# Gating the first weight slot once, norm means in single-pass matmuls, and a new order: a fused attention, GLU and SoLU kernel

## The chip, the cores and the metric

One core of one Trainium2 chip runs the whole program. The metric is the device time of one execution in microseconds; lower is better. TensorE (PE, with its weight loads PEld), VectorE (DVE), ScalarE (ACT), GpSimd (POOL) and the DMA engines work side by side and wait for each other by semaphores. SyncE (SP) only issues transfers.

## The reference, cut to what matters

```python
scores = q @ k^T / sqrt(64), masked to a window of 32 (half of the heads: dilated by 4)
attn = exp(scores - max) / (sum + 1e-9)
x = (attn @ v)                       # 4 x 8 heads x 576 x 64  ->  2304 tokens x 512
xn = x / sqrt(mean(x * x) + 1e-6) * rms_g
g = xn @ w_gate; val = xn @ w_val    # 512 x 1536
x = (g * sigmoid(g) * val) @ w_out   # 1536 x 512
h = x @ w_in                         # 512 x 1024
sm = exp(h - max) / (sum + 1e-9); solu = h * sm
ln = (solu - mean) / sqrt(var + 1e-6) * g_ln
out = ln @ w_out                     # 1024 x 512
```

The attention arrays are float32; the weight matrices and gains are float64, and the matrices reach the kernel as 64-bit words that it turns into fp32 itself.

## The kernel before, in words

The 2304 tokens are cut into nine tiles of 256 (`PIECES`, t = 0 to 8) and these into five parts (`PARTS`): tiles 0 and 1, tile 2, tiles 3 and 4, tiles 5 and 6, tiles 7 and 8. The hidden width 1536 is cut into twelve weight slots f of 128. Slot f brings three weight pieces of 128x512: gate (0), value (1), output (2).

**Weights** (`prepare`). A piece arrives as 64-bit words by one transfer of 512 KB (`fetch`, line 371). ScalarE shifts the exponent (`shifted`, line 386), VectorE takes low bits (`parts`, line 391) and joins both to fp32 (`joined`, line 395). ScalarE makes the fp32r high half (`halves`, a cast by the helper `put`, line 333) and VectorE or GpSimd subtracts it from the whole to get the low half (`lows`, helper `less`, line 342). The list `cuts` says which pieces are converted together: before, slots below `SINGLE` = 7 one by one, later slots all three as one 1536-wide step.

**Products.** A product of two fp32 arrays is three fp32r matmuls (`mm3`, lines 952 to 954): high x high, high x low, low x high. `mlp` makes g and vp (gate and value), then tanh, silu, product and the high and low halves of u, then y (the output product, accumulated over all slots). `VIRTUAL` lists its runs: entries 0 and 1 are slot 0 alone for tile 0 and tile 1 (256 columns each, so that tile 0 can start before tile 1 is ready), entry 2 is slots 1 to 11 for both (512 columns), entry 3 is tile 2, entry 4 tiles 3 and 4. Tiles 5 to 8 go through `joint`, a Strassen scheme of 512-column products whose operands are combined beforehand (`ewhole`, `ecomb`, `estore`: line 1240 is the combination, line 1244 its store). `second_stage` does the SoLU layer.

**Attention.** `pair` handles tiles 0 and 1 (scores lines 509 and 511, transposes 544, values 566), `attention` the later tiles (scores 639, transposes 675, values 695).

**Norms** (`rms`). Tiles 0 and 1 use small matmuls (line 820), a power on GpSimd, a diagonal and a spreading matmul (863). Tiles 2 to 8 square and add on GpSimd, then one fp32 matmul of a matrix of ones with the 128x256 sum gives each column's sum on all partitions (`mean`, line 827), then a Newton root on VectorE. `scale` (874, 879), `high` and `low` make the operands.

**What sets the order.** Each step is added to a `Plan` with a cost per engine, what it needs, the buffers that it takes and a due time. `Plan.order` plays the plan: it takes the engine that can start earliest, and on it, among the steps that can start within a small slack, the one that is due first. Each engine then runs its steps in that order, in its own in-order queue; SP issues transfers in the same way. `NUDGE` shifts the due times of single steps, `ENGINE` fixes the engine of some, `PACE` says behind which gate product a tile's attention may start. While GpSimd works, the plan charges VectorE for it: 0.45 of the GpSimd cost. From the joint products on TensorE's order is a written list (`line` in `second_stage`).

Up to planned time 75 us (`FILL`), the builder puts dummy matmuls (line 351, 256 columns of bf16 from a constant) into planned gaps of TensorE:

```python
filling[0] = int((at_ - free) / (0.13 if free else 0.25)) if at_ < FILL else 0
```

Of the kernel before, what the change touches and what calls it, by code (L numbers as in the profile page):

```python
# [7 lines left out]
F32 = mybir.dt.float32  # L8
F32R = mybir.dt.float32r
# [35 lines left out]
def groups_of(piece):  # L45
# [30 lines left out]
    else:  # L76
# [7 lines left out]
        for at, bt in ((128, b), (192, b2)):  # L84
# [12 lines left out]
HALVES = 1  # L97

# [4 lines left out]
SINGLE = 7  # L103
# [6 lines left out]
NUDGE = {('centred', (1, 1)): -15.5, ('copy', (1, 0)): 10, ('copy', (3, 1)): 11, ('copy', (4, 1)): 57,  # L110
         ('copy', (5, 0)): 32, ('copy', (7, 1)): 50, ('ecomb', 5): -17, ('eload', 9): 14, ('eps', 1): -41.9,
         ('eps', 3): 13, ('ewhole', 1, 0): -45, ('ewhole', 2, 1): 35, ('ewhole', 3, 0): 48, ('ewhole', 4, 0): 15,
         ('exps', (2, 1)): 57, ('g', 2, 8, 1): 24, ('gln',): 60, ('high', 0, 0): -27, ('high', 1, 0): 35,
         ('landed', 6): -22, ('load_qk', (1, 1)): -1.6, ('load_v', (0, 0)): 3.07, ('low', 0, 1): -43.6,
         ('low', 1, 0): 93, ('low', 1, 1): -32.8, ('masking', (2, 0)): -65, ('masking', (3, 1)): -22,
         ('masking', (4, 1)): 40, ('masking', (5, 0)): 13, ('masking', (6, 0)): -65, ('maximum', (1, 0)): -3,
         ('maximum', (1, 1)): -8.1, ('maximum', (2, 0)): -98, ('maximum', (3, 1)): -45, ('maximum', (5, 1)): 78,
         ('newton', 0, 2): 58, ('norm', (0, 1)): -0.8, ('norm', (2, 1)): 31, ('out', 2, 1, 0): -124,
         ('out', 2, 1, 1): 45.1, ('out', 2, 2, 0): 7.5, ('prod', 1, 0): 28, ('prod', 3, 0): 43, ('prod', 4, 3): 23,
         ('prod', 4, 7): 71, ('rmsg',): 14, ('scale', 0, 1): -35.9, ('scale', 1, 0): -11.5, ('scale', 1, 1): -38.4,  # L120
         ('scale', 1, 2): 0.08, ('scale', 1, 4): 1, ('scale', 2, 0): -5.5, ('scale', 2, 1): -25, ('scale', 2, 3): 49,
         ('scale', 3, 0): -11.4, ('scale', 3, 1): -38.8, ('scale', 3, 4): 43, ('silu', 3, 3): 17, ('silu', 3, 4): 46,
         ('square', 0, 0): 77, ('square', 0, 1): -34.9, ('square', 1, 1): -32.9, ('square', 1, 4): -10,
         ('square', 2, 1): -42.3, ('square', 3, 1): -29.9, ('sums', (1, 0)): -45, ('sums', (1, 1)): 44,
         ('tanh', 'c11', 0): 138, ('total', 2, 0): -12, ('total', 3, 0): -9.1, ('turned0', (0, 1)): -34,
         ('turned1', (0, 1)): -38, ('uhigh', 3, 4): -68, ('ulow', 4, 2): 88, ('ulow', 4, 4): 1, ('xcomb', 't3'): 35,
         ('xcomb', 't4'): 44, ('xlow', 't1', 1): 8, ((1, 0), 'lows', 0): 19, ((1, 0), 'lows', 1): 11,
         ((1, 0), 'shifted', 2): 33, ((1, 1), 'fetch', 0): 41, ((1, 1), 'fetch', 1): 12, ((1, 1), 'fetch', 2): 6,
         ((1, 1), 'joined', 0): 5.2, ((1, 1), 'joined', 2): -10, ((1, 1), 'lows', 2): -16.5,
         ((1, 1), 'parts', 1): 10, ((1, 1), 'parts', 2): 47.5, ((1, 1), 'shifted', 1): 91,  # L130
         ((1, 1), 'shifted', 2): 41, ((1, 10), 'fetch', 2): -33, ((1, 10), 'parts', 0): 23,
         ((1, 11), 'fetch', 0): -52, ((1, 11), 'fetch', 1): 31.9, ((1, 11), 'fetch', 2): -32,
         ((1, 11), 'lows', 0): 19.5, ((1, 11), 'parts', 0): 22.9, ((1, 2), 'fetch', 1): -5,
# [12 lines left out]

ENGINE = {('copy', (3, 0)): 'd', ('copy', (5, 0)): 'd', ('copy', (7, 0)): 'd', ('copy', (7, 1)): 'd',
          ('copy', (8, 1)): 'a', ('ecomb', 0): 'p', ('ecomb', 1): 'p', ('ecomb', 11): 'd', ('ecomb', 8): 'p',
          ((1, 4), 'lows', 0): 'p', ((1, 6), 'lows', 1): 'p'}

FILL = 75.0

# [1804 lines left out]
```

## Time and profile before

| | us |
|---|---|
| median of 3 runs (711.76 to 712.01) | 711.76 |
| the profiled execution | 712.27 |
| its span, first to last instruction | 710.2 |
| TensorE matmuls busy | 702.3 |
| VectorE, ScalarE, GpSimd busy | 509.4, 358.9, 135.5 |

The granted TensorE clock is 1.00 over the whole span. A matmul's recorded time includes its way through the pipeline, so two matmuls overlap in the records: what a matmul costs is read from the distance between two starts. An fp32 matmul shows as two records. Rows of the timeline merge instructions that follow each other with one line and shape.

### The profile page before, as it was taken

The page shows a single profiled execution, that of the slowest core. Times are in us where ns is not written, and L with a number is a line of the kernel's source. Part 1 is how long each engine was busy: PE and PEld are TensorE (multiplying, and loading weights), DVE is VectorE, ACT ScalarE, POOL GpSimd, SP SyncE. Part 2 cuts the span into 40 slices and gives each one's busy share as a digit, 9 for nine tenths or more (in the row PEclk, how much of TensorE's full clock was granted, in tenths as well). Part 3 has the DMA queues.
Part 4 walks back from the last instruction along what each step waited for, and adds up shares of the span by engine and source line. Part 5 has one row for each costly group of instructions (what it writes and reads, how often), then busy time and mean ns, then how long its engine had stood idle before and what let it go on. Part 6 is the DMA issues. An engine that isn't in the chain of part 4 may idle for free.

```text
span 710.2 us, 11738 instructions
## 1 busy us (share of the span) xinstructions
PE 702.3 (99%) x4533; PEld 593.3 (84%) x4533; DVE 509.4 (72%) x932; ACT 358.9 (51%) x769; POOL 135.5 (19%) x166
## 2 busy tenths in 40 slices
PE   8999999999999999999999999999999999999998
PEld 6788888899998888888888888888888888888887
DVE  5899899679585986668966766689677677665552
ACT  2976854344535554516655554355375555543440
POOL 0322432250506121110000000014044311010110
PEclk9999999999999999999999999999999999999999
DMA  9999433154368764403321112947032111000001
GB/s 336 401 407 354 133 101 118 64 185 141 134 225 293 276 206 141 141 7 125 123 72 37 52 60 97 344 139 220 1 119 75 60 60 45 30 16 30 30 30 45
DMA packets 42424, 97.21 MB, mean 137 GB/s; under 512 B 3841, under 2 KB 14081, under 8 KB 42369
## 3 DMA queue, kind: packets, MB, share of 16 engines
q1 hardware_dynamic: 40640, 93.33, 37.9%
q10 hardware_dynamic: 1728, 3.15, 1.2%
q8 instruction: 35, 0.57, 0.3%
q14 instruction: 21, 0.16, 0.1%
HBM read 72.87 MB, written 23.59 MB: 136 GB/s over the span
## 4 chain that ended last, share of the span: by engine, by line
PE 93%; DMA 5%; ACT 1%; DVE 1%; SPq 0%; issue 0%; ACTq 0%
PE y L952 7%; PE ca L1292 7%; PE y L954 7%; PE y L953 7%; PE o L1689 5%; PE o L1688 5%; PE o L1687 5%; PE g L952 4%; PE vp L952 4%; PE g L953 4%; PE g L954 4%; PE vp L954 4%; PE vp L953 4%; DMA raw<-w 3%; PE cd L1292 2%; PE cb L1292 2%
## 5 line engine op out<-in xcount | busy, mean ns | idle before, releaser
L342 POOL TENSOR_TENSOR w<-wf,w 128x512 fp32r<-128x512 f32 (+1 forms) x15 | 25.1, 1673 | 203.9 <-ACT w L333 203.9
L1687 PE MATMUL o<-w,lt 128*128 128x512 f32 (+1 forms) x152 | 58.9, 388 | 0.0
L1689 PE MATMUL o<-w,lt 128*128 128x512 f32 (+1 forms) x152 | 57.6, 379 | 0.0
L1688 PE MATMUL o<-w,lt 128*128 128x512 f32 (+1 forms) x152 | 57.5, 379 | 0.0
L952 PE MATMUL y<-uh,w 128*128 128x512 f32 (+1 forms) x148 | 53.2, 359 | 0.0
L954 PE MATMUL y<-uh,w 128*128 128x512 f32 (+1 forms) x148 | 51.7, 349 | 0.0
L953 PE MATMUL y<-uh,w 128*128 128x512 f32 (+1 forms) x148 | 51.7, 349 | 0.0
L660 ACT ACTIVATE s<-s,nm 128x64 f32<-128x64 f32 x120 | 40.1, 337 | 18.6 <-DVE nm L655 18.6
L333 ACT CAST w<-wf 128x512 fp32r<-128x512 f32 (+1 forms) x40 | 28.3, 728 | 25.5 <-DVE wf L395 11.5
L952 PE MATMUL g<-xh,w 128*128 128x512 f32 (+1 forms) x104 | 40.4, 389 | 0.0
L333 ACT CAST uh<-u 128x512 fp32r<-128x512 f32 (+1 forms) x37 | 19.9, 537 | 38.3 <-DVE u L996 37.7
L953 PE MATMUL g<-xl,w 128*128 128x512 f32 (+1 forms) x104 | 39.0, 375 | 0.2 <-DVE xl L342 0.2
L952 PE MATMUL vp<-xh,w 128*128 128x512 f32 (+1 forms) x100 | 39.0, 390 | 0.0
L954 PE MATMUL g<-xh,w 128*128 128x512 f32 (+1 forms) x104 | 38.9, 374 | 0.0
L954 PE MATMUL vp<-xh,w 128*128 128x512 f32 (+1 forms) x100 | 38.2, 382 | 0.0
L953 PE MATMUL vp<-xl,w 128*128 128x512 f32 (+1 forms) x100 | 38.1, 381 | 0.0
L805 POOL TENSOR_TENSOR sq<-x 128x256 f32<-128x256 f32 x28 | 17.8, 647 | 105.7 <-DVE x L337 61.6
L1655 POOL TENSOR_SCALAR st<-st 128x1 f32<-128x1 f32 x18 | 8.7, 484 | 140.5 <-ACT sq L1646 140.3
L992 DVE SCALAR_TENSOR_TENSOR u<-u,g 128x512 f32<-128x512 f32 (+1 forms) x37 | 21.5, 582 | 18.3 <-ACT u L986 18.3
L986 ACT ACTIVATE u<-g 128x512 f32<-128x512 f32 (+1 forms) x37 | 19.0, 514 | 27.9 <-PE g L954 27.2
L1689 PEld LDWEIGHTS o<-w,lt 128*128 128x128 f32 x152 | 28.6, 188 | 5.3
L342 DVE TENSOR_TENSOR lt<-tp,lt 128x512 fp32r<-128x512 f32 x36 | 23.2, 684 | 13.6 <-ACT lt L333 13.6
(290 smaller groups left out, 2056.5 us busy)
## 6 DMA issues: line engine op xcount, KB each, us to landing
raw<-w SPq DMA_DIRECT2D x36, 512.0 KB, 9.1
es<-ec SPq DMA_DIRECT2D x12, 512.0 KB, 3.1
sc<-es SPq DMA_DIRECT2D x12, 512.0 KB, 3.4
qk<-qk SPq DMA_DIRECT2D x7, 800.0 KB, 5.5
vt<-v SPq DMA_DIRECT2D x10, 512.0 KB, 5.6
wo<-w SPq DMA_DIRECT2D x9, 512.0 KB, 7.6
wst<-wo SPq DMA_DIRECT2D x9, 512.0 KB, 3.7
yT<-yo SPq DMA_DIRECT2D x16, 256.0 KB, 3.1
```

The source lines that it names most:

```text
L333: nc.scalar.copy(dst, src) if scale is None else nc.scalar.mul(dst, src, scale)
L342: ENG[e].tensor_tensor(dst, a, b, ALU.subtract)
L660: nc.scalar.activation(T[s_][:, i], T[s_][:, i], AF.Exp, bias=st["nm"][:, i:i + 1], accum_out=sm[:, i:i + 1])
L952: nc.tensor.matmul(acc, wh, xh, start=first, stop=False)
L953: nc.tensor.matmul(acc, wh, xl, start=False, stop=False)
L954: nc.tensor.matmul(acc, wl, xh, start=False, stop=last)
L986: return lambda e: nc.scalar.activation(new(up, ("u", v, f), [P, 512])[:, 0:n], T["g", v, f], AF.Tanh, scale=0.5)
L992: return lambda e: nc.vector.scalar_tensor_tensor(out=u_of(f), in0=u_of(f), scalar=1.0, in1=T["g", v, f], op0=ALU.add, op1=ALU.mult)
L1292: nc.tensor.matmul(acc(x), w, y, start=not more and j == 0 and n == 0, stop=j == 1 and n == 2, skip_group_check=True)
L1687: nc.tensor.matmul(o, lt[:, 0, k], w[:, 0], start=(k == 0), stop=False)
L1688: nc.tensor.matmul(o, lt[:, 0, k], w[:, 1], start=False, stop=False)
L1689: nc.tensor.matmul(o, lt[:, 1, k], w[:, 0], start=False, stop=(k == NF2 - 1))
```

## The change

Slot 0 gets no runs of its own any more. It joins the run of slots 1 to 11; its g and vp are done tile by tile (`by_piece`), its tanh, silu, product, halves and y once for 512 columns. The seven means of tiles 2 to 8 split the sum of squares into fp32r high (ScalarE) and low (GpSimd or VectorE) halves and use two fp32r matmuls. Slots 2 to 6 convert gate and value pieces as one 1024-wide step and the output piece apart; slots 0 and 1 stay in three, slots 7 to 11 in one. The mask matmul of `pair` becomes a step of its own. The plan's costs are adjusted, GpSimd's charge on VectorE is 0.45 only for steps that end in "low" or "lows" and 0.12 for others, and `NUDGE`, `ENGINE` and `PACE` are new lists.

```diff
-HALVES = 1
-SINGLE = 7
+APART, WIDE = 2, 7
+def cuts(f):
+    return [(0,), (1,), (2,)] if f < APART else [(0, 1), (2,)] if f < WIDE else [(0, 1, 2)]
...
-NUDGE = {('centred', (1, 1)): -15.5, ('copy', (1, 0)): 10, ('copy', (3, 1)): 11, ('copy', (4, 1)): 57,
+NUDGE = {('centred', (1, 1)): 39.5, ('copy', (1, 0)): 10, ('copy', (3, 1)): 11, ('copy', (4, 1)): 57,
...
+         ('ewhole', 4, 0): 15, ('ewhole', 5, 0): -132, ('ewhole', 5, 1): 103, ('exps', (2, 1)): 57,
+         ('g', 2, 8, 1): 24, ('gln',): 60, ('high', 0, 0): -6, ('high', 1, 0): 35, ('ident',): -462,
+         ('landed', 6): -116, ('load', 3): -176, ('load_qk', (1, 1)): -1.6, ('load_v', (0, 1)): 3,
+         ('load_v', (1, 0)): 6, ('low', 0, 1): -43.6, ('low', 1, 0): 93, ('low', 1, 1): -32.8, ('mask',): -119,
...
-          ('copy', (8, 1)): 'a', ('ecomb', 0): 'p', ('ecomb', 1): 'p', ('ecomb', 11): 'd', ('ecomb', 8): 'p',
-          ((1, 4), 'lows', 0): 'p', ((1, 6), 'lows', 1): 'p'}
+          ('ecomb', 2): 'p', ('ecomb', 5): 'p', ('ecomb', 7): 'd', ('ecomb', 8): 'p', ('high', 0, 0): 'a',
...
+          ((1, 2), 'lows', 1): 'p', ((1, 3), 'lows', 0): 'p', ((1, 4), 'lows', 0): 'p', ((1, 5), 'lows', 0): 'p',
+          ((1, 5), 'lows', 1): 'd', ((1, 7), 'lows', 0): 'p', ((1, 8), 'lows', 0): 'p'}
...
-PACE = {2: [(2, 3), (2, 2)],
-        3: [(2, 6), (2, 6)],
-        4: [(2, 8), (2, 10), (3, 1)],
-        5: [(3, 6), (3, 6)],
-        6: [(3, 9), (4, 0)],
-        7: [(4, 1), (4, 2)],
-        8: [(4, 3), (4, 4), (4, 6)]}
+PACE = {2: [(2, 0), (2, 7)],
+        3: [(2, 5), (2, 8)],
+        4: [(2, 2), (3, 1), (2, 7)],
+        5: [(3, 4), (3, 3)],
+        6: [(2, 3), (4, 2)],
+        7: [(3, 8), (3, 0)],
+        8: [(3, 6), (2, 0), (3, 10)]}
...
-VIRTUAL = [(0, 0, 256, range(HALVES)), (0, 256, 256, range(HALVES)), (0, 0, 512, range(HALVES, NF1)),
-           (1, 0, 256, range(NF1)), (2, 0, 512, range(NF1))]
+VIRTUAL = {2: (0, 0, 512, range(NF1)), 3: (1, 0, 256, range(NF1)), 4: (2, 0, 512, range(NF1))}
...
             if e == "p" and free["d"] > start:
-                free["d"] += 0.45 * cost
+                free["d"] += (0.45 if any(str(x).endswith(("low", "lows")) for x in name) else 0.12) * cost
...
         def mean(e):
             x = bank(a_mean, [P, TP], "ms")
-            nc.tensor.matmul(x, ones, T["sq", t, ks[0]], start=True, stop=True)
+            for h in range(2):
+                nc.tensor.matmul(x, ones_r, T["sqh" if h == 0 else "sql", t], start=h == 0, stop=h == 1)
+        def sum_high(e):
+            put(e, new(at, ("sqh", t), [P, TP], F32R, name="sqh"), T["sq", t, ks[0]])
+        def sum_low(e):
+            less(e, new(at, ("sql", t), [P, TP], F32R, name="sql"), T["sq", t, ks[0]], T["sqh", t])
...
+                    fill(T[key][:, 0:TP])
+                else:
+                    filling[0] = 3 * filling[0] // 4
+                    if v == 2 and filling[0] > 0:
+                        fill(psy.tile([P, 512], F32, tag="y00", name="warm")[:, 0:TP])
...
-                    alone = v == 4 and f == 0 and part == 0
+                    alone = f == 0 and (v == 2 or v == 4 and part == 0)
+                    if alone and part == 1:
+                        before = [("g", v, f, i)] + ([(key, v, f, 0)] if i else [])
```

## Rows read from the trace of the kernel before

**Rows 1.** The page, part 1: busy time (share of the span) and instructions
```profile
PE 702.3 (99%) x4533; PEld 593.3 (84%) x4533; DVE 509.4 (72%) x932; ACT 358.9 (51%) x769; POOL 135.5 (19%) x166
```

**Rows 2.** Stages: length; PE, PEld, DVE, ACT, POOL busy (instructions); PEclk, DMA share, GB/s
```profile
0.00:36.66 36.66, 32.41 (x410) 25.56 (x410) 24.67 (x55) 22.48 (x41) 6.26 (x15) 1.00 0.98 370
36.66:80.00 43.34, 43.34 (x295) 36.72 (x296) 41.28 (x64) 30.99 (x61) 12.33 (x9) 1.00 0.84 321
80.00:196.00 116.00, 116.00 (x992) 104.27 (x991) 91.63 (x157) 56.24 (x170) 39.32 (x41) 1.00 0.37 127
196.00:198.00 2.00, 1.47 (x13) 1.30 (x13) 1.90 (x6) 0.60 (x3) 0.00 (x0) 1.00 0.77 213
198.00:706.00 508.00, 508.00 (x2821) 424.64 (x2821) 349.45 (x652) 248.55 (x499) 77.60 (x102) 1.00 0.32 107
```

**Rows 3.** Stages, line 351 alone: length; PE, PEld busy (instructions); PEclk, DMA share, GB/s
```profile
29.18:36.66 7.48, 3.14 (x25) 2.32 (x25) 1.00 1.03 397
36.66:710.20 673.54, 0.00 (x0) 0.00 (x0) 1.00 0.36 124
```

**Rows 4.** Timeline of PE around one mean: start us, us, engine line op out<-in xcount
```profile
107.19 0.39 PE L953 MATMUL y<-uh,w 128*128 128x512 f32 x1
107.42 0.39 PE L954 MATMUL y<-uh,w 128*128 128x512 f32 x1
107.65 0.59 PE L827 MATMUL ms<-sq,ones 128*128 128x256 f32 x2
...
108.31 0.39 PE L953 MATMUL g<-xl,w 128*128 128x512 f32 x1
```

**Rows 5.** Timeline of PE, the last slot-0 products and the first of slot 1
```profile
39.52 0.28 PE L952 MATMUL y<-uh,w 128*128 128x256 f32 x1
...
40.96 0.40 PE L952 MATMUL g<-xh,w 128*128 128x512 f32 x1
```

**Rows 6.** Timeline of all engines, how tile 1 (the second token piece) becomes ready
```profile
33.22 1.66 DVE L879 SCALAR_TENSOR_TENSOR x<-x,rmsg,rs 128x256 f32<-128x256 f32 x4 [0.19 <-PE rs L863]
...
34.69 0.68 ACT L386 ACTIVATE raw<-raw 128x512 f32<-128x512 f32 x1 [0.38 <-DMA raw<-w]
...
35.28 1.12 ACT L333 CAST xh<-x 128x512 fp32r<-128x512 f32 x2
35.92 1.29 DVE L342 TENSOR_TENSOR xl<-x,xh 128x512 fp32r<-128x512 f32 x2 [0.71 <-ACT xh L333]
...
36.11 0.36 PE L952 MATMUL g<-xh,w 128*128 128x256 f32 x1
...
36.66 0.38 PE L953 MATMUL g<-xl,w 128*128 128x256 f32 x1 [0.19 <-DVE xl L342]
```

**Rows 7.** Timeline of DVE and POOL: subtractions alone and beside GpSimd
```profile
38.52 0.42 DVE L342 TENSOR_TENSOR uh<-u,uh 128x256 fp32r<-128x256 f32 x1
...
39.35 0.69 DVE L342 TENSOR_TENSOR w<-wf,w 128x512 fp32r<-128x512 f32 x1
...
41.43 1.30 POOL L342 TENSOR_TENSOR w<-wf,w 128x512 fp32r<-128x512 f32 x1 [6.19 <-ACT w L333]
...
41.69 1.32 DVE L342 TENSOR_TENSOR uh<-u,uh 128x256 fp32r<-128x256 f32 x1
```

**Rows 8.** Groups by line and form, the means: busy us, mean ns | idle before
```profile
L827 PE MATMUL ms<-sq,ones 128*128 128x256 f32 x14 | 4.2, 378 | 0.0
```

**Rows 9.** Timeline of SP's queue: the first two issues
```profile
0.73 0.46 SPq L486 DMA_DIRECT2D qkv<-qk  x1
1.24 0.45 SPq L1839 DMA_DIRECT2D masks<-mask  x1
```

**Rows 10.** Timeline around the hole: start us, us, engine line op, idle before and releaser
```profile
191.72 1.14 ACT L333 CAST xh<-x 128x512 fp32r<-128x512 f32 x2 [4.12 <-DMA es<-ec]
...
196.30 0.28 PE L954 MATMUL vp<-xhl,w 128*128 128x256 f32 x1
...
197.10 0.63 PE L675 MATMUL tp<-ident,s 128*128 128x128 f32 x4 [0.53 <-DVE s L668]
```

More of the change, by code (lines that the diff above doesn't have):

```diff
@@ L495, in scores, with masked @@
             fill(x.rearrange("p s k -> p (s k)"))
+            for y in range(2):
+                for i in range(4):
+                    for c in range(2):
+                        b = 4 * (i // 2) + 2 * c + i % 2
+                        k0 = 512 + g["offs"][b]
+                        nc.tensor.matmul(x[64 * c:64 * c + 64, 4 * y + i, :], qk()[:, y, 64 * b:64 * b + 64],
+                                         qk()[:, y, k0:k0 + 64], start=y == 0 and i == 0, stop=False)
+        def masked(e):
+            x = T[sp]
             n = g["mask"]
@@ L589, in pair @@
         plan.add(step("weights"), {"d": 0.7}, weights, [step("norm")], uses=[s_], due=due)
-        plan.add(step("transposes"), {"t": 0.66}, transposes, [step("weights")], takes=[(banks[1], tp)], uses=[s_], due=due)
+        plan.add(step("transposes"), {"t": 0.5}, transposes, [step("weights")], takes=[(banks[1], tp)], uses=[s_], due=due)
         for r in range(2):
@@ L758, in attention @@
             needs_, takes_, uses_ = for_values(K)
-            plan.add(step("values"), {"t": 0.27 + 0.465 * N}, values, needs_, takes=takes_, uses=uses_, due=due)
-        cost = 0.7 if N == 2 and g["kind"] != "tail" else 0.5 * N
-        plan.add(step("copy"), {"d": cost, "a": cost}, copy,
+            plan.add(step("values"), {"t": 0.2 + 0.485 * N}, values, needs_, takes=takes_, uses=uses_, due=due)
+        a, d = (0.62, 0.7) if g["kind"] == "plain" else (0.85, 1.05) if N == 2 else (0.65, 0.6)
+        plan.add(step("copy"), {"d": d, "a": a}, copy,
                  [step("values") if K not in LEADS else ("scores", LEADS[K])] + ([("copy", (t, 0))] if m else []) +
@@ L903, in rms @@
         for k in ks:
-            plan.add(step("square", k), {"a": 0.42} if stays else {"a": 0.42, "d": 0.42, "p": 0.75} if first else {"p": 0.7},
+            plan.add(step("square", k), {"a": 0.42} if stays else {"a": 0.42, "d": 0.42, "p": 0.75} if first else {"p": 0.64},
                      square(k), [("values", (t, source[k] // 2))] if stays else
@@ L1257, in group_ @@
             else:
-                add(("eload", q), {"s": 1.35}, plain, [((1, f), "kept", 0 if f >= SINGLE else X) for f in fs] + (first or [("vp", 3, NF1 - 1, 1)]),
+                add(("eload", q), {"s": 1.35}, plain, [((1, f), "kept", 0 if f >= APART else X) for f in fs] + (first or [("vp", 3, NF1 - 1, 1)]),
                     takes=[("ec2", ec)] + rooms * (q == NF1 // 2), uses=held, due=50 + q)
@@ L1709, in second_stage @@
         add = plan.add
-        mm, base = 0.2265, 6000
+        mm, base = 0.2271, 6000
         def switch(e):
@@ L1855, in tile_attention_glu_solu @@
                 ([("low", k, 0) for k in range(2)] + [("values", K) for K in EARLY] if f == X_AT else []))
-    for v in range(len(VIRTUAL)):
+    for v in VIRTUAL:
         mlp(v, 1000 * (v + 1))
```

169 lines of the change are left out of this document (89 added, 80 removed), and 8 rows, old and new, of tables (ENGINE, NUDGE).

## The prediction

> **What bounds the kernel now.** I read the page's busy shares first: TensorE is busy for 702.3 of the 710.2 us span, VectorE 72%, ScalarE 51% [rows 1]. A share that high can be padding, so I asked next for busy time by stage and for the dummy matmuls (line 351, which keep the engine from standing still while there is no real work). By stage TensorE is full from 36.66 us to 706 us except for a hole near 196 us [rows 2]. Dummies: 3.14 us of them lie between the first real gate matmul (29.18 us) and 36.66 us, and none behind that [rows 3]. So the span has three parts: a start to 36.66 us, set by attention, norms and weight conversion on ScalarE and VectorE; 669.5 us of real matmuls with one hole; and a tail behind the last matmul that the change does not touch. DMA is at 98% of its engines in the start but only 36% afterwards [rows 2, 3]. The reader should take from this: behind 36.66 us only removed TensorE work or a removed TensorE wait shortens the kernel, and ahead of it only an earlier readiness of the second token piece does.
>
> **Norm means.** Tiles 2 to 8 each have one mean, so seven. Before, one fp32 matmul of 256 columns is recorded as two passes. From the y matmul at 107.42 us to the second g matmul at 108.31 us are 0.89 us [rows 4]; two ordinary slots of 0.227 us (107.19 to 107.42) belong to y and g, which leaves 0.89 - 0.45 = 0.43 us for the mean. After, it is two fp32r matmuls of 256 columns; twelve such matmuls stand between 39.52 and 40.96 us, 0.12 us each [rows 5], together 0.24 us. Gain 0.19 us each, 7 x 0.19 = 1.3 us, all of it on the full engine. It could come out at nothing only if this matmul were not run like the others of its type and width, whose pace those rows show.
>
> What it adds lies beside: a cast of 128x256 on ScalarE, at most the 0.56 us of one of 512 (two in 1.12 us) [rows 6], and a subtraction of 128x256, 0.42 us on VectorE when alone [rows 7], or on GpSimd; 7 x 0.56 = 3.9 us and 7 x 0.42 = 2.9 us on engines with 49% and 28% of the span free [rows 1]. They are hidden by other tiles' matmuls, as long as the mean stands late enough in TensorE's order. It stands in an in-order queue: if the subtraction is late, all matmuls behind wait. Without that cover each mean would cost up to 0.56 + 0.42 = 1.0 us, seven of them 6.9 us; I take nothing, since the means of before have 0.0 us of idle time ahead of them [rows 8], although theirs is the same queue and the same wait.
>
> **First weight slot.** Before, slot 0 runs g, vp and y for 256 tokens twice. After, g and vp still run piece by piece, y once with 512 columns: 24 matmuls x 0.12 = 2.88 us become 12 x 0.227 = 2.72 us, gain 0.16 us. Of the element-wise steps, VectorE's three are done once at 512 instead of twice at 256, by its rows 3 x (2 x 0.42 - 0.69) = 0.45 us less in the tight start [rows 7]. What is lost is cover: y of piece 0 (12 x 0.12 = 1.44 us, from 39.52 to 40.96) stood ahead of slot 1's gate matmul [rows 5]. Without it TensorE wants slot 1's gate weights at 39.5 us; the subtraction that finishes them, as I read the order of weights, runs from 39.35 to 40.04 us [rows 7]. That is a wait of 0.5 us with the pace of before. The y of slot 0 now comes behind slot 1's two products (2 x 2.72 us), longer than its element-wise chain, so it waits for nothing new.
>
> **Order of the start.** Today piece 1 releases TensorE at 36.66 us. Its operands went: scaling by VectorE from 33.22 us, then ScalarE's cast at 35.28 us, which stood behind a weight shift that waited for a transfer until 34.69 us, then VectorE's subtraction at 35.92 us [rows 6]. Two of four scalings (each a quarter of 1.66 us) suffice for the first cast, so it could begin at 34.1 us: 1.2 us earlier. What is late next is then the scaling itself. The nudges move transfers: identity and mask now go ahead of the first query block, which was issued at 0.73 us in 0.46 us, with the next issue at 1.24 us [rows 9]; two issues of 0.5 us delay it by 1.0 us on SP's queue, and with it the first scores. By the due times the first value load of tile 0 moves forward, ahead of tile 1's queries, and the others back behind them, two of them with weights ahead; today's waits of tile 0's products on values are not on piece 1's path, so nothing. Scores no longer wait for the mask, which arrives first anyway: nothing. Bounds for the start: best, all dummies between 29.18 and 36.66 us (3.14 us) and the wait on the piece's operands (36.11 to 36.66, less one slot: 0.43 us) [rows 3, 6] vanish, a gain of 3.6 us; worst, 1.0 us later issue plus the 0.5 us of slot 1, a loss of 1.5 us. I take the row that is nearest, the removed head-of-line wait less slot 1's wait: 1.2 - 0.5 = 0.7 us gain.
>
> **Two-block weights.** Slots 2 to 6 convert gate and value weights in one 1024-wide step. VectorE is busy for 41.28 of 43.34 us between 36.66 and 80 us [rows 2], so fewer fixed costs help it, but TensorE does not wait there now, so on the path it is nothing. What covers the coarser step: weights run ahead, as DMA's share shows. If that cover is gone, g of slot 2 waits for vp's conversion.
>
> **The hole.** At 197.10 us transposes wait for VectorE's softmax weights; the last matmul ahead of them began at 196.30 us, 0.80 us earlier where a slot is 0.12 us, so the hole is 0.68 us [rows 10]. Behind it: ScalarE stood 4.12 us for a store of combined weights before it cast x, and the exponentials queued behind [rows 10]. The new order starts those combinations much earlier (nudge -132) but moves them to GpSimd. Between 0 and 0.68 us; I take 0.68, since the wait that caused it is what moves; its last 0.7 us is all that must go. Next late would be the vp matmuls' own operands, which are there.
>
> **Second half.** TensorE's list from the joint products on is written out by hand and is unchanged; it is full now [rows 2], so other engine choices there bring nothing unless they open a wait.
>
> **A rule against the change.** At 41.69 us a 128x256 subtraction on VectorE took 1.32 us instead of 0.42 us (38.52 us), while GpSimd's subtraction of 128x512 ran from 41.43 to 42.73 us [rows 7]. The new order pins weight subtractions up to 1536 wide on GpSimd. The Trainium skill, SBUF — State Buffer, section Who interferes with whom, says that a VectorE instruction with two SBUF inputs and a GpSimd instruction that reads SBUF exclude each other for the whole instruction; this trace agrees (VectorE ended 0.3 us after GpSimd). By that rule the sum is larger by as many wide blocks as TensorE has no cover for; by the rows, TensorE had no wait behind such a block, and I add nothing.
>
> **Sum.** 1.3 + 0.16 + 0.7 + 0.68 = 2.84 us. The profiled execution took 712.27 us (2.1 us outside its span) and becomes 709.4 us; the median of the runs, 711.76 us, is 0.5 us lower and becomes 708.9 us.
>
> **The rivals.**
> - The start is packed fully: 3.6 us instead of 0.7 us gained, 708.9 - 2.9 = 706.0 us. For it: of the 7.48 us between 29.18 and 36.66 us, 3.14 us are dummies [rows 3]. Against: ScalarE and VectorE have 22 and 25 us of work there [rows 2], and slot 1's weights would have to be earlier too. Chance 0.20.
> - Gains hidden: the hole stays, slot 1's and slot 2's weights come late (0.5 us plus about 1 us), the start gains nothing: 711.76 - 1.46 + 1.0 = 711.3 us. For it: VectorE 95% full after 36.66 us. Chance 0.20.
> - Slower: VectorE becomes the bound between 36.66 and 80 us, because it is shut out behind 1024-wide GpSimd subtractions: 2.5 us each by scaling the 1.30 us of 512. A blocked y operand or weight costs TensorE 2.5 us, less its cover. Two uncovered blocks (5.0 us) with the later first issue (1.0 us) outweigh the 1.46 us of removed matmul time: 711.8 + 4.5 = 716.3 us; one block and the issue give 713.8 us, so it decides from one uncovered block on. VectorE has only 43.34 - 41.28 = 2.06 us free in that stretch, and behind each blocked instruction of its in-order queue stand the softmax and gating steps that TensorE waits for; against it, the same lock costs TensorE nothing today. Chance 0.10.
> - The single-pass mean is not single pass: each of its two matmuls costs 0.43 us, seven means lose 3.0 us instead of gaining 1.3 us: 713.2 us. That the type does not bring what it says would be the cause; the pace of the others speaks against it [rows 5]. Chance 0.04.
>
> **The numbers.** The forecast, 708.9 us, has 0.46; its own range, with the hole kept at one end and 1 us more of start at the other, is 707.5 to 710.3 us. The range that leaves out the slower two rivals and the best packed end is 705.5 to 711.9 us. A measurement of this kernel tells about 0.2% (1.4 us) from no change, so faster means below 710.3 us and slower above 713.2 us. Faster: 0.44 of the forecast, 0.20, and little of the hidden case, 0.65. Same: 0.22. Slower: 0.13.
>
> **What would show it.** Right: means as 14 records of fp32r with slots of 0.12 us; no y matmul of 256 columns in slot 0; first full stretch of TensorE starting near 36 us with slot 0's work done earlier; no wait near 197 us. Wrong: waits on VectorE's subtraction or GpSimd's between 38 and 80 us, dummies behind 37 us, a mean that waits for its subtraction, or a new wait of attention's transposes or exponentials between 140 and 310 us.

## The result, and the profile of the changed kernel

The changed kernel is slower: 719.2 us (median of 4 runs, 719.10 to 719.26) against 711.9 us for the kernel before on the same chip, a ratio of 1.010 with a 95% interval of 1.0082 to 1.0117. The forecast was 708.9 us with a range to 711.9 us, so both the sign and the range were wrong.

The page of the changed kernel (busy shares; the costliest group with a wait: busy us, mean ns | idle before it and its releaser) looks much like [rows 1], and one row in it is new:

```profile
PE 703.9 (98%) x4528; PEld 593.4 (83%) x4528; DVE 514.5 (72%) x926; ACT 364.1 (51%) x770; POOL 136.4 (19%) x156
...
L997 PE MATMUL y<-uh,w 128*128 128x512 f32 (+1 forms) x144 | 52.0, 361 | 4.0 <-DVE uh L372 4.0
```

TensorE's y matmuls stood idle 4.0 us in all for one VectorE step, the subtraction that makes the low half of u (line 372; it was line 342 before); 3.6 us of it are one wait at 90 us. Busy time by stage (length; PE, PEld, DVE, ACT, POOL busy; granted clock, DMA share, GB/s) shows where, beside [rows 2]:

```profile
0.00:38.71 38.71, 33.14 (x417) 26.05 (x417) 25.51 (x55) 21.08 (x38) 5.52 (x15) 1.00 0.97 359
38.71:90.00 51.29, 51.21 (x267) 42.67 (x265) 49.50 (x53) 37.66 (x60) 24.28 (x13) 1.00 0.72 283
90.00:98.00 8.00, 4.40 (x13) 3.17 (x13) 7.90 (x7) 1.55 (x2) 3.43 (x1) 0.79 0.00 0
98.00:716.00 618.00, 615.14 (x3838) 521.48 (x3836) 431.63 (x813) 303.84 (x673) 103.14 (x129) 1.00 0.33 111
```

The second piece releases TensorE at 38.71 us instead of 36.66 us. TensorE is then full up to 90 us, half idle for 8 us, and full again. Within these 8 us, the timelines of VectorE and GpSimd read:

```profile
85.81 7.62 POOL L372 TENSOR_TENSOR w<-wf,w 128x1536 fp32r<-128x1536 f32 x2 [3.27 <-ACT w L363]
...
86.34 3.81 DVE L421 TENSOR_SCALAR raw<-raw 128x1536 uint32<-128x1536 uint32 x1
90.07 3.91 DVE L372 TENSOR_TENSOR uh<-u,uh 128x512 fp32r<-128x512 f32 x1
```

Two weight subtractions, each 1536 wide (the low parts of slots 11 and 7), run back to back on GpSimd from 85.81 to 93.43 us (3.52 and 4.16 us). Beside them a VectorE operation that takes 0.95 us when alone lasts 3.81 us, and the 512-wide subtraction for which TensorE waits lasts 3.91 us instead of 0.69 us [rows 7]. TensorE's timeline of the same place, and its granted clock (the last but two of the columns, in stretches of 2 us):

```profile
90.05 0.39 PE L996 MATMUL y<-uh,w 128*128 128x512 f32 x1
94.03 0.79 PE L997 MATMUL y<-uh,w 128*128 128x512 f32 x1 [3.60 <-DVE uh L372]
...
95.05 0.63 PE L996 MATMUL y<-uh,w 128*128 128x512 f32 x1
95.48 0.63 PE L997 MATMUL y<-uh,w 128*128 128x512 f32 x1
...
97.49 0.39 PE L996 MATMUL y<-uh,w 128*128 128x512 f32 x1
```

```profile
92.00:94.00 2.00, 0.00 (x0) 0.00 (x0) 2.00 (x2) 0.00 (x0) 1.43 (x1) 0.98 0.00 0
94.00:96.00 2.00, 1.97 (x5) 1.58 (x6) 1.90 (x3) 0.60 (x1) 0.00 (x0) 0.50 0.00 0
96.00:98.00 2.00, 2.00 (x8) 1.58 (x7) 2.00 (x3) 0.95 (x2) 0.00 (x0) 0.67 0.00 0
```

From one y matmul to the next are 3.98 us, 3.76 us more than a slot. Behind the wait the clock is granted at 0.50, that is 1.2 GHz, and the matmuls come every 0.43 us: eight slots take 3.46 us (94.03 to 97.49) instead of 8 x 0.227 = 1.82 us, 1.64 us more. Wait and clock together are 5.4 us.

**Where 7.1 us of span went.** Start to the second piece: 38.71 - 36.66 = +2.05 us. From there to the first joint product (324.55 us before, 330.83 us after): +4.23 us, of which +5.4 us are the block above, +0.58 us a wait of y for VectorE at 157.53 us, -1.19 us the means, -0.69 us the hole that is gone and -0.16 us slot 0's y; 0.3 us stay unassigned. (38.71 us is the start of the second piece's first matmul; before, 36.11 us was, and the second one stood in a wait until 36.66 us. Counted at the last of the piece's twelve g matmuls, 40.21 against 37.96 us, the start is 2.25 us late, and 0.1 us stays unassigned.) From the first joint product to the end: +0.82 us, 0.45 us of it a wait at 357.8 us and 0.32 us a longer tail.

The start in the order of its events, beside [rows 6] (the spread 2.0 us later, the scaling 2.0 us, the cast 1.2 us, and one of the two subtractions now on GpSimd, where it takes 1.84 us):

```profile
34.48 0.70 PE L903 MATMUL rs<-rd,ones 128*128 128x256 f32 x2 [1.61 <-DVE rd L369]
35.22 1.65 DVE L919 SCALAR_TENSOR_TENSOR x<-x,rmsg,rs 128x256 f32<-128x256 f32 x4 [0.46 <-PE rs L903]
36.51 1.14 ACT L363 CAST xh<-x 128x512 fp32r<-128x512 f32 x2 [2.95 <-DVE x L919]
37.73 1.84 POOL L372 TENSOR_TENSOR xl<-x,xh 128x512 fp32r<-128x512 f32 x1 [3.58 <-ACT xh L363]
...
38.71 0.36 PE L996 MATMUL g<-xh,w 128*128 128x256 f32 x1
```

One sentence for what follows: in some executions of these kernels TensorE's granted clock is 0.50 for 2 to 6 us of the start, which costs up to some 2 us (a mean clock of 0.997 in some runs of the kernel before fits that), so medians within 0.5 us of each other are not told apart below, and one execution of e16 that took 1424.7 us is not counted in its ratio.

### The profile page after: what moved, and what is told of

Its sections match the earlier page's. It is cut to its first block, busy times and chain, and to the rows that moved or that the text cites. A ratio compares the mean times of both kernels' runs of the same rounds, so it can differ in the third digit from the quotient of the medians.

```text
span 717.3 us, 11702 instructions
## 1 busy us (share of the span) xinstructions
PE 703.9 (98%) x4528; PEld 593.4 (83%) x4528; DVE 514.5 (72%) x926; ACT 364.1 (51%) x770; POOL 136.4 (19%) x156
## 4 chain that ended last, share of the span: by engine, by line
PE 86%; DVE 7%; DMA 4%; issue 1%; ACT 1%; POOL 0%; SPq 0%; DVEq 0%; ACTq 0%; POOLq 0%
PE y L997 7%; PE y L996 6%; PE y L998 6%; PE ca L1339 6%; PE o L1735 5%; PE o L1734 5%; PE o L1736 5%; PE g L996 3%; PE g L998 3%; PE vp L996 3%; PE g L997 3%; DMA raw<-w 3%; PE vp L997 3%; PE vp L998 3%; PE pv L728 2%; PE tp L1715 2%
## 5 line engine op out<-in xcount | busy, mean ns | idle before, releaser
L363 ACT CAST w<-wf 128x512 fp32r<-128x512 f32 (+2 forms) x35 | 28.0, 804 | 24.3 <-DVE wf L425 9.2
L372 POOL TENSOR_TENSOR w<-wf,w 128x512 fp32r<-128x512 f32 (+2 forms) x14 | 33.7, 2418 | 32.2 <-ACT w L363 30.1
L372 POOL TENSOR_TENSOR wf<-wf 128x512 f32<-128x512 f32 x3 | 4.7, 1568 | 168.1 <-DVE wf L1483 162.1
L997 PEld LDWEIGHTS y<-uh,w 128*128 128x128 f32 x144 | 27.6, 192 | 8.3 <-DVE uh L372 4.6
```

Of the source, the lines that this page charges most:

```text
L363: nc.scalar.copy(dst, src) if scale is None else nc.scalar.mul(dst, src, scale)
L372: ENG[e].tensor_tensor(dst, a, b, ALU.subtract)
L997: nc.tensor.matmul(acc, wh, xl, start=False, stop=False)
```

## The experiments

All were compared with the kernel before on the same chip. "Lows" are the subtractions that finish a weight slot.

### The block at 90 us

**e1_lows_on_vector.** The two wide lows go to VectorE, at the same places of the order:

```diff
+ELSEWHERE = {((1, 11), 'lows', 0): 'd', ((1, 7), 'lows', 0): 'd'}
 for at_, _, name, e in plan.play():
+    e = ELSEWHERE.get(name, e)
```

> The changed kernel with two 1536-wide weight subtractions (slots 11 and 7) done by VectorE instead of GpSimd, at the same place of the order; nothing else moves. Theory 'shut out' (VectorE loses 2 x about 3 us because GpSimd holds the SBUF port for the whole of a 3.7 us instruction, and TensorE then waits 3.8 us at 90 us and runs 8 matmuls at the lower clock, 1.7 us): both go, 719.2 - 5.5 = about 713.7 us, although VectorE gets 3.5 us more work. Rival 'VectorE has too much work in that stretch': 3.5 us more of it makes the wait longer, 720 us or more.

Measured: 713.97 us, ratio 1.003 (1.0017 to 1.0043). VectorE does 3.5 us more work and the kernel is 5.2 us faster than the changed one. Its VectorE timeline has the same operations at their plain lengths, and TensorE is full there at a clock of 1.00:

```profile
86.39 1.75 DVE L372 TENSOR_TENSOR w<-wf,w 128x1536 fp32r<-128x1536 f32 x1
88.06 0.95 DVE L421 TENSOR_SCALAR raw<-raw 128x1536 uint32<-128x1536 uint32 x1
88.93 0.68 DVE L372 TENSOR_TENSOR uh<-u,uh 128x512 fp32r<-128x512 f32 x1
```

**e2_lows_in_thirds.** The lows stay on GpSimd, cut into pieces of 512:

```diff
-less(e, th[:, :, 1], wf_(c), th[:, :, 0])
+for j in range(len(c)) if e == "p" else ():
+    less(e, th[:, j, 1], wf_(c)[:, j], th[:, j, 0])
```

> The changed kernel, with every GpSimd weight subtraction that is wider than 512 cut into instructions of 512, still on GpSimd; no work moves between engines. Theory 'shut out for a whole instruction': VectorE can get in between the thirds, each of its blocked instructions waits at most about 1.3 us, the wait at 90 us shrinks from 3.8 us to under 1.5 us and the low clock goes: 714 to 715.5 us. Rival 'the two engines share the port, so that each is slowed as long as both run': the cut changes nothing or adds fixed cost, 719 to 720 us.

Measured: 714.84 us, ratio 1.004 (1.0025 to 1.0055). GpSimd is busy even longer (10.68 us for six pieces), but VectorE gets in between them, and the wait at 90 us is gone:

```profile
86.01 10.68 POOL L372 TENSOR_TENSOR w<-wf,w 128x512 fp32r<-128x512 f32 x6 [3.27 <-ACT w L363]
...
86.55 1.59 DVE L421 TENSOR_SCALAR raw<-raw 128x1536 uint32<-128x1536 uint32 x1
88.09 1.73 DVE L372 TENSOR_TENSOR uh<-u,uh 128x512 fp32r<-128x512 f32 x1
```

So what counts is not GpSimd's total work beside VectorE but the length of the single instruction that VectorE has to sit out. A new wait of 1.33 us, from 109.2 us on, keeps this kernel behind e1.

**e12_other_low_on_vector.** Only slot 7's low goes to VectorE; slot 11's stays on GpSimd, alone.

> The kernel after with only slot 7's low on VectorE; slot 11's 1536-wide low stays on GpSimd at 85.8 us. Theory 'a GpSimd subtraction shuts VectorE out for as long as it lasts, and only two in a row reach TensorE': VectorE's operation on raw still lasts over 3 us beside it, but the subtraction of uh takes 0.7 us and ends near 90.3, TensorE waits under 0.5 us at 90 us and its clock stays up: about 714 us. Rival 'any 1536-wide subtraction on GpSimd in this block costs its length': the wait stays 2 us or more, 717 us or more.

Measured: 715.67 us (714.9 to 716.4), ratio 1.0055 (1.0041 to 1.0068); the profiled execution also has clock falls in the start.

```profile
86.47 3.51 POOL L372 TENSOR_TENSOR w<-wf,w 128x1536 fp32r<-128x1536 f32 x1 [3.27 <-ACT w L363]
...
87.00 3.80 DVE L421 TENSOR_SCALAR raw<-raw 128x1536 uint32<-128x1536 uint32 x1
90.71 0.68 DVE L372 TENSOR_TENSOR uh<-u,uh 128x512 fp32r<-128x512 f32 x1
```

```profile
90.68 0.39 PE L996 MATMUL y<-uh,w 128*128 128x512 f32 x1
91.45 0.50 PE L997 MATMUL y<-uh,w 128*128 128x512 f32 x1 [0.38 <-DVE uh L372]
```

One wide subtraction still makes VectorE's 0.95 us operation last 3.80 us, but TensorE then waits 0.54 us beyond its slot and the clock stays at 1.00 there. Two in a row are what made the loss: the second one caught the operation that TensorE needed. In the median the kernel is 1.7 us behind e1. The two traces are 2.5 us apart: 0.6 us up to the second piece, 1.4 us from there to the first joint product, with longer waits at 90 and 110 us, and 0.5 us behind it.

**e3_dummies_in_wait.** 33 dummy matmuls ahead of the waiting y block, to see what the clock alone costs:

```diff
+if name == ("out", 2, 5, 0):
+    filling[0] = 33
```

> The changed kernel with 33 dummy matmuls (3.7 us) ahead of the y product that waits at 90 us. Theory 'the wait costs twice, once by itself and once by the lower clock behind it': the wait stays, the granted clock stays at 2.4 GHz, the eight slow matmuls are gone, 719.2 - 1.7 = about 717.5 us. Rival 'the slots of 0.43 us behind the wait are something else (late operands, weight loads)': no change, 719.2 us, or up to 0.5 us longer if the dummies overshoot.

Measured: 719.17 us (717.88 to 720.16), ratio 1.010: no gain in the median. In the block itself the clock stayed at 1.00 and the slots at 0.23 us; what the profiled execution lost again, it lost in the start, where the clock was 0.50 from 32 to 38 us (one of these stretches is shown first):

```profile
34.00:36.00 2.00, 1.80 (x6) 1.62 (x7) 1.02 (x4) 0.00 (x0) 0.00 (x0) 0.50 1.03 413
...
92.00:94.00 2.00, 2.00 (x21) 1.76 (x19) 2.00 (x1) 0.00 (x0) 2.00 (x1) 1.00 0.00 0
94.00:96.00 2.00, 2.00 (x16) 1.57 (x14) 1.90 (x2) 0.00 (x0) 0.75 (x1) 1.00 0.00 0
```

The two runs of the four with the higher mean clock (717.88 and 718.3 us) are about 1.1 us below 719.2 us. That the idle time brought the clock down is shown in the block. Its price shows in the stretch behind the start: from the second piece's first matmul to the first joint product are 290.54 us here and 292.12 us in the changed kernel, 1.6 us less, as the eight slow slots say. In the median it does not show.

### The start

**e4_loads_as_before.** The first 14 transfers in the order of the kernel before, all else as after.

> The changed kernel, the first 14 transfers issued in the order of the kernel before (first query block ahead of mask and identity, all four query blocks ahead of the value loads and weights); all compute steps keep their order. Theory 'the late second token piece is due to the order of the first transfers': its scores come 3 us earlier, the second piece is ready 1.5 to 2.1 us earlier, 717.1 to 717.7 us. Rival 'the start is set by the order on ScalarE and VectorE': under 0.4 us, 718.8 to 719.2 us.

Measured: 721.67 us, ratio 1.0135, worse than after. The second tile's scores came earlier (14.04 instead of 16.36 us for its second pair), but the second piece did not: 38.88 us. The theory of the loads fell, and this trace shows why:

```profile
17.95 0.43 DVE L421 TENSOR_SCALAR raw<-raw 128x512 uint32<-128x512 uint32 x1 [2.10 <-DMA raw<-w]
18.30 0.68 DVE L547 TENSOR_REDUCE nm<-sp 128x8 f32<-128x512 f32 x1
...
17.95 0.69 ACT L416 ACTIVATE raw<-raw 128x512 f32<-128x512 f32 x1 [2.80 <-DMA raw<-w]
```

The maximum of the second tile's last scores (line 547) could have begun near 16 us, when they were there. It stood 2.10 us behind a step of slot 0's weight conversion that waited for its transfer; ScalarE's exponentials stood behind the other such step. The new order has two gates in a row, late loads and waiting conversion steps, and opening one does not help. The loss against the changed kernel lies behind the start, 1.55 us of it in a new wait that ends at 70.5 us, for a weight's subtraction on GpSimd. From here on the start was tried on the kernel of e1.

**e8_queue_order** puts the softmax ahead of those conversion steps and leaves the loads; **e9_queue_order_and_loads** does both:

```diff
+AT = {('maximum', (1, 1)): 17.08, ((1, 0), 'shifted', 0): 18.65, ('sums', (1, 0)): 18.66,
...
+steps.sort(key=lambda x: (AT.get(x[2], x[0]), x[1]))
```

> The kernel after with the lows of slots 11 and 7 on VectorE (so 713.97 us is what it is measured against) and, at the start, the second tile's softmax put ahead of slot 0's weight conversion in the queues of ScalarE and VectorE; SyncE's loads stay as they are. Theory 'two gates in a row' (the second tile's queries and keys come late, at 16.1 us, and a conversion step that waits for its weight stands ahead of the softmax; each gate alone is enough to hold the second piece back): next to nothing, the second piece starts at 38.2 to 38.7 us, time 713.4 to 714.3. Rival 'queue order alone': the second piece starts at about 36.7 us, time 712.2. Rival 'the engines are simply full': no change or a later second piece, 714 or more.

> The same as the run before it, and also the first 14 transfers in the order of the kernel before. Theory 'two gates in a row': with both gates open the fourth pair's maximum starts near 16 us instead of 18.3, the root of the second tile some 1.8 us earlier, the second piece at 36.5 to 37.0 us instead of 38.5; time 712.2, if no weight that is loaded later comes late (the earlier run with this order of loads had such a wait of 1.55 us near 69 us; with it 713.7). Rival 'the engines are simply full': second piece not before 38 us, 714 or more.

Measured: e8 718.03 us, ratio 1.0088, second piece at 42.67 us. Alone, the new order made TensorE stand 1.75 us at 22 us; the clock was then 0.50 from 24 to 30 us. e9: 714.13 us (712.85 to 715.27), second piece at 38.23 us. The maximum did begin at 16.28 us, but only 0.3 us came through, because a third gate stood behind the two, a cast of slot 0's weight that waited for VectorE ahead of the squares of the norm:

```profile
20.92 0.62 ACT L363 CAST w<-wf 128x512 fp32r<-128x512 f32 x1 [1.10 <-DVE wf L425]
21.44 0.83 ACT L832 ACTIVATE sq<-pv 128x256 f32<-128x256 f32 x2
```

Both expectations of mine were wrong: e8 was thought harmless, e9 sufficient.

**e13_second_tile_first** moves every conversion step of slot 0 behind the second tile's softmax and squares.

> As the last run of the start (lows of slots 11 and 7 on VectorE, the first 14 transfers as in the kernel before), and now every conversion step of slot 0 behind the second tile's softmax, its squares and its turned rows on ScalarE and VectorE: in the last run the cast of slot 0's weight still stood in front of the squares on ScalarE and waited 1.10 us for VectorE, so TensorE waited 0.98 us at 21 us and only 0.3 us was won. Theory 'several gates in a row, each enough alone': second piece at 36.4 to 36.9 us (38.2 in the last run), time 712.4 (711.6 to 713.0). Rival 'ScalarE and VectorE are simply full in the start, the order only moves the wait': second piece not before 37.8 us, or a weight of slot 0 comes late in its place; 713.7 or more.

Measured: 714.42 us, ratio 1.0045, second piece at 38.95 us, so the rival is right for this order: the conversion, pushed back, now stood ahead of the first tile's norm on VectorE, and the spread that needs it kept TensorE waiting (1.35 us at 25.9 us). This trace has a clock of 0.50 from 32 to 34 us besides, so not all of its start is the order.

**e16_start_as_before** takes the order and engines of the kernel before for all steps up to the second piece, not only for the few I had picked; **e17_nothing_ahead** also puts four conversion steps of slots 1 and 2 behind the second tile's norm:

> The kernel after with the lows of slots 11 and 7 on VectorE (713.97 us), and all steps of attention, norm, loads and slot 0's conversion up to the second piece in the order and on the engines that they have in the kernel before; what stays of the change in the start is its substance: the slot 0 by pieces one after the other, its matmuls behind the norm's spread, early weights by two blocks. Theory 'the order of the searched start is what costs 2 us': second piece at 36.5 to 37.0 us (38.7 after, 36.7 before), time 713.97 - 1.8 = 712.2 (711.5 to 712.7). Rival 'the substance costs it (one gate for both pieces, two-block weights crowd the engines whatever the order)': second piece at 38 us or later, 713.7 or more.

> As the run with the start in the old order, and four conversion steps of slots 1 and 2, which in that run stood ahead of the second tile's norm and waited for their own weight (VectorE 30.99 to 33.36 us ahead of the diagonal, ScalarE 36.12 us ahead of the second piece's high half), put behind it. Theory 'conversion steps ahead of the second tile's norm in the queues': diagonal at 31.5, spread at 32.4, second piece at 36.4 to 37.0 us; time 712.3 (711.6 to 712.8) where the clock stays up in the start. Rival 'the substance costs it': with the first piece's matmuls behind the spread TensorE has nothing but filler between 30 and 33 us, its granted clock falls as in the last run's profile (0.50 at 32 to 36 us) and takes the gain: second piece at 38 or slots of double length there, 713.5 or more.

Measured: e16 714.27 us, ratio 1.0026 (1.0015 to 1.0037); its profiled execution has the second piece at 39.87 us with the clock at 0.50 from 32 to 36 us, and again three conversion steps ahead of the norm's diagonal on VectorE, the first waiting for its transfer:

```profile
30.99 2.46 DVE L421 TENSOR_SCALAR raw<-raw 128x512 uint32<-128x512 uint32 x3 [0.61 <-DMA raw<-w]
33.36 0.47 DVE L369 TENSOR_SCALAR rd<-ident,r 128x128 f32<-128x128 f32 x2
```

e17: the second piece is at 36.84 us, against 36.66 us before, inside the bounds of the theory. The diagonal starts at 31.08 us:

```profile
31.08 1.49 DVE L369 TENSOR_SCALAR rd<-ident,r 128x128 f32<-128x128 f32 x2 [0.88 <-POOL r L893]
...
36.84 0.36 PE L996 MATMUL g<-xh,w 128*128 128x256 f32 x1
```

So the order, with the engines of a few steps, is what made most of the start late, and not the joint slot 0 or the two-block weights: at the last g matmul of the second piece 1.6 of the 2.25 us are back (40.21 us in the changed kernel, 38.59 us here, 37.96 us before). The other 0.6 us stay open. The time did not follow as far: 713.69 us, ratio 1.0028 (1.0018 to 1.0039), where 712.3 us was expected. Span against e1: 1.67 us won up to the second piece, 0.8 us of it given back between the first joint product and the end (386.1 us there in e1, 386.9 us in e17, with a wait of 0.46 us at 440.1 us that e1 has not). Against the kernel before 1.1 us of span remain, although the means and the hole are gained (+0.6 us up to that g matmul, -0.8 us from there to the first joint product, +1.3 us behind it): waits at 106.7 us (0.41 us) and 150.8 us (0.58 us), those at 351 and 440 us, and many of some 0.1 us. I did not trace these further.

### The means and the hole

**e14_one_fp32_mean.** e1 with one fp32 matmul per mean again; the split of the squares is still made and nobody reads it.

> The kernel after with the lows of slots 11 and 7 on VectorE (713.97 us), the seven means made by one fp32 matmul again; the split of the squares is still made, at its old place, and read by nobody. If the prediction's term for the means is right in size and lies on the path: 7 x 0.19 = 1.3 us slower, 715.3 (714.9 to 715.7). Rival 'the gain is hidden behind other waits': under 0.4 us, 714.3 or less.

Measured: 715.88 us (715.25 to 716.75) against 713.97 us. Of these 1.9 us, the seven means themselves account for 1.19 us: reckoned as in [rows 4], they hold TensorE for 3.03 us here as in the kernel before, and for 1.84 us with single-pass matmuls. The traces agree: from the second piece to the first joint product this one is 1.16 us longer than e1's. Most of the rest is start: this kernel's profiled execution has a clock of 0.60 from 24 to 28 us, and its second piece is 0.8 us later than e1's. Five of the seven single-pass means take 0.24 us, as in this pair of the changed kernel (0.12 us to the second, 0.12 us to the next matmul); the two that stand right behind transposes take 0.33 us.

```profile
165.18 0.28 PE L861 MATMUL ms<-sqh,ones_r 128*128 128x256 f32 x1
165.30 0.28 PE L861 MATMUL ms<-sql,ones_r 128*128 128x256 f32 x1
165.42 0.28 PE L996 MATMUL g<-xhl,w 128*128 128x256 f32 x1
```

**e10_before_single_pass.** The kernel before with the seven means alone changed, high half on ScalarE and low half on VectorE; the split enters the order 1 us behind the last addition, and the means with the norm steps behind them move back by 1 us too:

```diff
-nc.tensor.matmul(x, ones, T["sq", t, ks[0]], start=True, stop=True)
+for h in ("sqh", "sql"):
+    nc.tensor.matmul(x, ones_r, T[h, t], start=h == "sqh", stop=h == "sql")
...
+put("a", T["sqh", t], s)
+less("d", T["sql", t], s, T["sqh", t])
```

> The kernel before, everything in its old order, with only the seven means cut into two single-pass matmuls (high half on ScalarE, rest on VectorE, the mean and the steps up to the Newton rounds planned 1 us later). If the prediction's term for the means holds: two matmuls of 0.118 us each in the place of one of 0.43 us, 7 x 0.19 = 1.3 us, so 712.0 - 1.3 = 710.7 (710.3 to 711.1), a version that beats both kernels. Rival 'the split is late and TensorE waits for it': a wait before some of the means, 712 or more.

Measured: 716.49 us, ratio 1.0069 (1.0057 to 1.0082): the rival, and 5.8 us above my number. ScalarE reaches the high half only behind a block of exponentials, VectorE stands waiting for it, and the softmax of the next pair stands behind VectorE; TensorE then waits 0.90 us for that softmax. Five more such new waits, 0.34 to 1.12 us, stand between 162 and 292 us, two of them at the mean near 195 us.

```profile
255.27 0.43 DVE L343 TENSOR_TENSOR sql<-sq,sqh 128x256 fp32r<-128x256 f32 x1 [2.28 <-ACT sqh L334]
...
256.88 0.30 PE L676 MATMUL tp<-ident,s 128*128 128x128 f32 x1 [0.74 <-DVE s L669]
```

**e18_split_on_gpsimd, e19_split_and_hole, e20_hole_alone.** e18: the kernel before with both halves of the split on GpSimd, right behind its last addition. e20: the kernel before with the two casts of the hole [rows 10] behind the exponentials. e19: both. In e18 the mean and the step behind it move back where the split needs it. The first lines of the diff are against e10, the last one is that of e19 and e20.

```diff
-put("a", T["sqh", t], s)
-less("d", T["sql", t], s, T["sqh", t])
+put("p", T["sqh", t], s)
+less("p", T["sql", t], s, T["sqh", t])
...
+AT = {('high', 0, 3): 194.90, ('high', 1, 3): 194.91, ('low', 0, 3): 194.92}
```

> The kernel before with the seven means cut into two single-pass matmuls, and now both halves of the split on GpSimd right behind its last addition, so that no other queue stands waiting for them. Theory 'place': no new waits ahead of the attention's transposes, 711.9 - 1.3 = 710.6 (710.2 to 711.2). Rival 'substance' (two more operations per norm always delay something): new waits of TensorE again, 712.5 or more.

> The same with the two casts of the next piece, which wait for a store near 188 us, put behind the exponentials on ScalarE: if the hole's cause was read rightly, the wait of 0.69 us near 197 us goes and the time is 709.9 (709.4 to 710.6), faster than both kernels; if the cast is needed in its place, a later wait takes its room, 710.6 or more.

> The kernel before with only those two casts moved: 711.9 - 0.7 = 711.2 if the cast that waits for the store is the cause of the hole; 711.9 or more if it is not.

Measured: e18 712.89 us, 1.0013 (1.0004 to 1.0021); e19 714.21 us, 1.0038; e20 712.07 us, 1.0006 (0.9997 to 1.0015). e20's transposes follow their matmul at once, so the hole's cause was read rightly, yet the time did not move. In the profiled execution the gain is there and lost again: from the sixth g matmul of the second piece to the first joint product it is 0.6 us shorter than the kernel before, and the start, with a clock of 0.50 from 32 to 34 us, is 0.8 us longer. In the executions with a mean clock of 1.000 the gain does not show either (spans of 709.8 us in the median, 709.6 us for the kernel before on the same chip); why stays open.

```profile
197.08 0.28 PE L954 MATMUL vp<-xhl,w 128*128 128x256 f32 x1
197.20 0.60 PE L675 MATMUL tp<-ident,s 128*128 128x128 f32 x4
```

In e18 the first mean now waits for GpSimd twice (0.32 and 0.69 us beyond the slots), and there is a new wait of 0.58 us at 164 us:

```profile
108.40 0.38 PE L833 MATMUL ms<-sqh,ones_r 128*128 128x256 f32 x1 [0.16 <-POOL sqh L336]
109.21 0.38 PE L833 MATMUL ms<-sql,ones_r 128*128 128x256 f32 x1 [0.43 <-POOL sql L343]
```

In e19 the two edits met, and the effect of 90 us came back. The casts, moved back, bring GpSimd's two 512-wide subtractions of the next piece to 197.08 us, beside the last steps of a softmax that VectorE could only begin after a wait for the mean. Two of these take 0.87 and 1.49 us instead of 0.30 and 0.69 us in e18, and the transposes behind them, at 200.33 us, waited 1.9 us. Neither expectation held.

```profile
197.08 2.56 POOL L343 TENSOR_TENSOR xl<-x,xh 128x512 fp32r<-128x512 f32 x2 [1.79 <-ACT xh L334]
...
198.69 1.49 DVE L673 TENSOR_TENSOR s<-s,rn 128x512 f32<-128x512 f32 x1
```

**e21_split_settled.** e18 with the first mean 1 us later on TensorE and three scales of the fourth piece behind the activation that they delayed:

```diff
+AT = {('mean', 2): 109.6, ('scale', 0, 3): 163.6, ('scale', 1, 3): 163.61, ('scale', 3, 3): 163.62}
```

> The kernel before with the split on GpSimd, the first mean 1 us later on TensorE and three scales of the fourth piece behind the activation they delayed on VectorE. If the two waits were all that ate the gain: 712.89 - 0.98 - 0.58 = 711.3 (710.8 to 711.7), below both kernels. Rival 'each cure moves the wait on': 712.2 or more.

Measured: 711.13 us (710.83 to 713.32, 11 runs) against 712.17 us, ratio 0.9988 (0.9979 to 0.9997): faster than both kernels, by 1.0 us. Both waits are gone; the hole is still there, 0.53 us long, and the means hold TensorE for 2.23 us, 0.8 us less than before. From the second piece to the first joint product its trace is 1.4 us shorter than that of the kernel before; what the means do not explain of that was not traced.

## Why the prediction was wrong

**The step that failed** is the one under "A rule against the change": "by the rows, TensorE had no wait behind such a block, and I add nothing". The runs put about 5 us in its place: 5.4 us by the trace, 5.2 us by e1. The row that I trusted showed one 512-wide block and a cover that happened to be there. The trace of before held the price as well, and I did not read it: a VectorE operation of 0.42 us lasts 3.61 us beside a 1536-wide subtraction, and TensorE has no wait behind it. VectorE's next subtraction of u ends at 125.97 us, 0.5 us ahead of the y matmul that reads a low half (126.49 us):

```profile
120.55 3.62 POOL L342 TENSOR_TENSOR w<-wf,w 128x1536 fp32r<-128x1536 f32 x1 [13.73 <-ACT w L333]
...
120.84 3.61 DVE L843 SCALAR_TENSOR_TENSOR rt<-rsb,rd 128x256 f32<-128x256 f32 x1
```

The mechanism stood among the rivals, at a chance of 0.10, with 1024-wide blocks between 36.66 and 80 us. Those came, four of them, 2.41 to 2.87 us each, and cost TensorE nothing: it is busy for 51.21 of the 51.29 us up to 90 us. What cost was two of 1536 in a row, 3.52 and 4.16 us, and what tipped it was their sequence (e12). The rule of the Trainium skill (SBUF — State Buffer, section Who interferes with whom: VectorE and GpSimd take the shared ports for a whole instruction) stood there and was weighed at nothing. Here the trace agrees with it, at 0.95 us becoming 3.8 us, and e2 confirms the words "whole instruction". The same page says that a one-input VectorE operation joins in when it runs in a two-port mode; the tensor_scalar on raw, stretched like the subtraction, fits that, though no run here tests which mode it was in.

**A term that I did not have at all:** TensorE's clock after a wait. Behind 3.76 us of idle time slow matmuls lost 1.64 us; e3 shows the clock at 1.00 when dummies fill the wait, and 1.6 us back. The Trainium skill, TensorE: Matmul & The Clock Gate, section Part 1: The HAM clock gate, says that the clock follows how busy the engine has been; this agrees.

**Order of the start:** predicted 0.7 us earlier, measured 2.05 us later, outside my worst bound of 1.5 us. I looked for one head-of-line wait ([rows 6]) and assumed that the new order only removes it. I priced the later loads at one queue's issue time and "today's waits" at nothing, and did not ask which conversion steps the new order puts ahead of the softmax on ScalarE and VectorE. The runs name the cause of most of it: conversion steps that wait for their own weight, ahead of the second tile's softmax and norm, in series with the later loads (e4, e9, e16), and with the old order the second piece is back at 36.84 us (e17). The clock plays no part in it: the changed kernel's own profile has 1.00 up to 38.71 us.

**Norm means:** right in kind and nearly in size, 1.19 us for 1.3 us. But taking nothing for the split holds only for its place: in the changed kernel it hides; on the kernel before the same means made anything from 1.0 us of gain (e21) to 4.7 us of loss (e10), depending on the queue in which the split stood and on what stood behind it.

**First slot, 0.16 us, and the hole, 0.68 us:** both there in the trace. The 0.5 us wait for slot 1's gate weights, which the start's term took off, is not: score matmuls of a later tile run in its place, and slot 1's first g matmul loses 0.27 us at 43.09 us. The hole's cause was right (e20); that its removal is a gain of the whole kernel was not shown.

**Two-block weights and the second half:** taken at nothing. No run takes the two-block conversion out by itself; TensorE has no wait for it up to 90 us. Behind 100 us new waits of 0.58 us (y for VectorE's subtraction, 157.53 us) and 0.45 us (a joint product for ScalarE, 357.8 us) opened. They are not the waits of transposes or exponentials that the prediction named as a sign there. Behind the first joint product the changed kernel is 0.8 us longer than before, e17 1.3 us.

**Sums.** The forecast's own range, 707.5 to 710.3 us, does not come out of the two terms that it names, which give 707.9 and 709.6 us. Scaling 1.30 us to 1024 columns gives 2.6 us, not 2.5, and from 36.66 to 706 us are 669.3 us, not 669.5. None of them changes the outcome.

## What to carry to other kernels

When work moves to GpSimd, price each of its instructions as time in which VectorE may do nothing, and look for the consumer two VectorE instructions on: subtractions back to back are the dangerous form, while single ones were often free, and cutting them, or giving them to VectorE, was worth 4 to 5 us here. Read also where such a block costs nothing today: it has the same length there, and only what stands behind it differs. In a start with in-order queues, a step that waits for a transfer is a gate for all behind it; several such gates in a row hide each other, so take the whole old order back first and only then single steps. A saving on the full engine counts only if the work that feeds it stands in a queue where nobody waits for it.

## What was not expected of the hardware

A VectorE operation with one input tensor, in place on 32-bit integers, was held up by GpSimd like one with two: 0.95 us became 3.80 and 3.81 us beside a 1536-wide GpSimd subtraction that by itself took 3.51 us. GpSimd is slowed by the sharing too: six pieces of 512 took 10.68 us in e2, 1.78 us each, where [rows 7] has 1.30 us for one. Not every VectorE operation is held: in e2 the step from g to u (line 1036), whose input g TensorE writes, kept its 0.67 us at 89.75 us beside one of these pieces.
